# h of the four-block units turned by a DMA transpose on the load queue, in a training step of a gated long convolution

## The chip, the core and the metric

The kernel runs on one core of a Trainium2 chip. The metric is the device time of one execution in microseconds, as the median of the runs. The engines that matter are TensorE (PE: matmuls and transposes, results in PSUM), VectorE (DVE: elementwise work), ScalarE (ACT: activations and most copies out of PSUM), GpSimd (POOL) and SyncE (SP, which here only issues DMAs). SP, ACT and POOL each issue DMAs in the order of their own queue, and a DMA whose condition is not met holds up whatever stands behind it on that queue.

## The reference

The outputs are the forward result and the gradients of all operands of

```
xn  = layernorm(A_q)                                   # 2048 x 1024
kv  = shift_conv(A_k, A_shift_k) * A_v
s   = xn * (long_conv(kv, A_ssm_k) + kv * A_ssm_D)     # FFT convolution over 2048 rows
g   = xn @ w_gate;  u = xn @ w_up;  h = g * u          # 2048 x 3584
bm  = h @ w_down
out = A_q + s * silu(bm)
```

The gradient of w_down needs h with the rows of the sequence on the partitions, and h @ w_down needs h turned, with the features on the partitions. So the kernel writes both forms of h to DRAM: `Hd` as it is computed and `HTd` turned.

## The kernel before, in words

Everything is bf16 with sums in fp32. The 2048 rows are 16 blocks of 128 (`NB`), the 3584 features 14 slabs of 256 (`SLW`, `NSL`).

*The first stage* runs to about 528 us and does two things at once. `gu_unit` computes g and u for one slab and a run of blocks: four blocks in 54 of the units, one or two blocks in six early ones (the first 512 rows of slabs 0 and 1). For each block there are eight matmuls of 128x512 (line 661) that put u and g side by side into one PSUM tile `psg`, and a ScalarE copy to `gut` (line 663). At the end of a unit ScalarE's queue stores `gut` to `GUd` (line 670). Between the blocks the call `tick()` at line 669 emits pieces of `conv_forward`, the long convolution as discrete Fourier transforms: short matmuls into `psF` (line 235) and `psY` (lines 438 and 449), ScalarE copies of `psF` to `SP` (lines 257 and 295), and very much VectorE work (all of it through `tt`, line 213, on tiles W, KX, HX, m, U). How much is emitted at each tick is worked out from estimated VectorE weights, so the order of TensorE's, VectorE's and ScalarE's work is fixed at build time; most of these instructions are pinned to program order. The spectra go to DRAM from GpSimd's queue, `KFd<-KX` among them.

*What happens to h.* In the first block of the next unit `multiply` makes `hN` = u * g on VectorE (line 675; three buffers) and GpSimd's queue stores it to `Hd` (line 676). `multiply` puts `turn` on the list `later`. `flush(5)`, called once per block at line 664, adds one to the age of each entry and runs those that have reached 5. `turn` (lines 685 to 692) turns the eight 128x128 squares of a unit with TensorE against the identity into a PSUM tile (line 690), copies it to `hT` with ScalarE (line 691; two buffers), and `store` writes it to `HTd` on SP's queue (line 682, issued through `ld`, line 61).

*SP's queue* in this stage also carries the slab loads (`wslab`, line 540, two buffers, issued about a slab ahead) and, near the end, the pieces of w_down (`WD[0]` to `WD[6]`, `load_wd`) and the first loads of `HTd`.

*The second stage*, h @ w_down, begins at 519 us with `bm_first` (line 989): TensorE goes over 28 chunks `fc` of 128 features for two row blocks at a time (four matmuls of 128x512 per chunk, line 985); chunk fc reads `WD[fc // 4]`. A flush at line 1002 after its first four chunks runs what is left on `later`. `WD[6]` lies in a buffer of a pool that is allocated only when the pools of the first stage, `hT`'s among them, are released. After each pair of blocks `gate` does the elementwise part (its first VectorE instruction on a result is gg, on bm and sig). Behind this come the two stages of the gate and up gradients, the gradient of w_down and that of the layer norm, up to 1929 us.

Of the kernel before, what the change touches and what calls it, by code (L numbers as in the profile page):

```python
# [19 lines left out]
def build_kernel(  # L20
# [11 lines left out]
    nc = tc.nc  # L32
# [27 lines left out]
    def ld(out, in_):  # L60
        return nc.sync.dma_start(out=out, in_=in_)
# [3 lines left out]
    def st(out, in_):  # L65
        ins = nc.gpsimd.dma_start(out=out, in_=in_)  # L66
        if PINQ[0]:
            tc.keep_in_program_order(ins)
        return ins

    def sta(out, in_):
        return nc.scalar.dma_start(out=out, in_=in_)
# [139 lines left out]
    def tt(o, a, b, op):  # L212
        pinned(V.tensor_tensor(o, a, b, op))  # L213
# [401 lines left out]
    def turn_late():  # L615
        for i, (x, q, qi) in enumerate(turn_rows):
            ps = ps_st.tile([P, DC, P], BF16, name="tr")
            for dc in range(DC):
                tr_ln[0] = nc.tensor.transpose(ps[:, dc, :], x[:, dc * P:(dc + 1) * P], ident[:])
            if i % 2 == 0:  # L620
                act_copy[0] = nc.scalar.copy(out=XNT[q][:, :, qi * P:(qi + 1) * P], in_=ps[:])
            else:
                V.tensor_copy(XNT[q][:, :, qi * P:(qi + 1) * P], ps[:])
        turn_rows.clear()
# [3 lines left out]
    later = []  # L628
    gu_mm = [None]

    def defer(fn):
        later.append([0, fn])

    def flush(age=0):

        for e in later:
            e[0] += 1
        while later and later[0][0] >= age:
            later.pop(0)[1]()
# [5 lines left out]
    def gu_unit(sl, b0, n, w, tick):  # L645

        if n == 4:
            turn_of[0] += 1
            if turn_of[0] % 3 == 0 and sl < NSL - 2:
                gut = U[5][:, 2048:4096].rearrange("p (a i f) -> p a i f", a=2, i=4)  # L650
            else:
                gut = fg.tile([P, 2, 4, SLW], BF16, name="gut")
            hN = fg.tile([P, 2, 4, P], BF16, name="hN", bufs=3)
        else:
            gut = lnp.tile([P, 2, 2, SLW], BF16, name="gut_s", bufs=6)
            hN = lnp.tile([P, 2, 2, P], BF16, name="hN_s", bufs=6)
        for i in range(n):
            q, qi = divmod(b0 + i, 4)
            ps = ps_gu.tile([P, 512], F32, name="psg")
            for dc in range(DC):  # L660
                gu_mm[0] = nc.tensor.matmul(ps[:], XNT[q][:, dc, qi * P:(qi + 1) * P],  # L661
                                            w[:, dc].rearrange("p a f -> p (a f)"), start=(dc == 0), stop=(dc == DC - 1))
            nc.scalar.copy(out=gut[:, :, i], in_=ps[:].rearrange("p (a f) -> p a f", a=2))  # L663
            flush(5)
            if i == 0:
                turn_late()
            hn[0]()
            hn[0] = nop
            tick()
        sta(GUd[sl, b0 // 8][:, :, b0 % 8:b0 % 8 + n], gut[:, :, 0:n])  # L670

        def multiply():
            with tc.issue_after(last.ins) if b0 + n <= 4 and chunk[0] <= 2 else nullcontext():
                by_half = lambda t: t.rearrange("p i (a f) -> p a i f", a=2)
                tt(hN[:, :, 0:n], by_half(gut[:, 0, 0:n]), by_half(gut[:, 1, 0:n]), MUL)
            st(Hd[sl][:, :, b0:b0 + n, :], hN[:, :, 0:n])
            defer(turn)
        hn[0] = multiply

        def store(hT):  # L680
            fr, so = sl % 12 * SLW, b0 % 8 * P
            ld(HTd[b0 // 8][sl // 12][fr:fr + SLW, so:so + n * P].rearrange("(a f) s -> f a s", f=P),
               hT[:, :, 0:n].rearrange("f a i s -> f a (i s)"))

        def turn():
            hT = fg.tile([P, 2, 4, P], BF16, name="hT") if chunk[0] > 5 else lnp.tile([P, 2, 4, P], BF16, name="hT_s", bufs=5)
            ps = ps_tr.tile([P, 2, 4, P], BF16, name="tr")
            for a in range(2):
                for i in range(n):
                    nc.tensor.transpose(ps[:, a, i, :], hN[:, a, i, :], ident[:])  # L690
            nc.scalar.copy(out=hT[:, :, 0:n], in_=ps[:, :, 0:n])
            store(hT)
# [239 lines left out]
    def tick(by=1):  # L932
        cnt[0] += by
        if cnt[0] == -4:
            pump((SHIFT_W + 4.05) / F_TOTAL)
        if cnt[0] >= -2:
            pump((SHIFT_W + (F_TOTAL - SHIFT_W) * (cnt[0] + 6.5) / (NT + 3.5)) / F_TOTAL)
# [265 lines left out]
    def gate(b, ps):  # L1203
# [36 lines left out]
        if b >= 12:  # L1240
            defer(turn)
# [406 lines left out]
```

## Time and profile before

| what | before |
|---|---|
| median of 3 runs | 1930.18 us (1929.89 to 1932.31) |
| the profiled execution, span | 1929.5 us |
| TensorE busy | 1906.4 us, 10843 matmuls and transposes |
| VectorE busy | 1549.6 us |
| ScalarE busy | 638.4 us |
| GpSimd busy | 330.5 us |
| DMA moved | 444 MB, mean 230 GB/s |

The page cuts the span into 40 slices of 48 us. A digit is the busy share of a slice in tenths; the first 11 slices are the first stage.

```profile
PE   8999999999999999999999999999999999999999
DVE  9999999999937556888899999999996404288884
ACT  5764555555422233343222222222212102011113
PEclk9999999999999999999999999999999999999999
DMA  8876866758899997666788788575787999889985
```

The turning itself appears on the page in these DMA issues (out<-in, queue, count, KB each, median us from issue to landing):

```profile
Hd<-hN POOLq DMA_DIRECT2D x54, 256.0 KB, 4.0
ht<-HTd SPq DMA_DIRECT2D x6, 1536.0 KB, 11.4
```

A matmul is counted as busy for its whole length although the next one starts before it ends: the 128x512 matmuls last 379 ns each and start 216 ns apart when nothing holds them up.

### The profile page before, as it was taken

To read this page: it belongs to the slowest core of one execution; us is meant where nothing else is said; L and a number is where in the kernel's file an instruction comes from. 1 tells how busy PE (TensorE), PEld (TensorE's weight loads), DVE (VectorE), ACT (ScalarE), POOL (GpSimd) and SP (SyncE) were. 2 spreads that over 40 slices of the span, in tenths; PEclk is the share of its full clock that TensorE was granted. 3 is DMA by queue.
4 is the path that set the end of the run, shared out by engine and by line. 5 is a ranking of instruction groups with operands and counts; after the bars stand their busy time and mean duration, and the time that the engine had idled before them with its cause. 6 is when DMAs were issued, how large, how long until landed. Compare 5 with 4: busy or idle time off the path is not lost.

```text
span 1929.5 us, 27354 instructions
## 1 busy us (share of the span) xinstructions
PE 1906.4 (99%) x10843; PEld 1031.0 (53%) x10978; DVE 1549.6 (80%) x1730; ACT 638.4 (33%) x942; POOL 330.5 (17%) x461
## 2 busy tenths in 40 slices
PE   8999999999999999999999999999999999999999
PEld 5555555555444456665666666664444444444444
DVE  9999999999937556888899999999996404288884
ACT  5764555555422233343222222222212102011113
POOL 4121212111112210000122131121211101011111
PEclk9999999999999999999999999999999999999999
DMA  8876866758899997666788788575787999889985
GB/s 293 268 259 217 261 209 226 234 196 268 272 270 311 282 313 258 208 202 219 258 246 261 239 248 262 202 272 174 226 253 174 157 205 210 153 170 201 191 177 169
DMA packets 451361, 444.43 MB, mean 230 GB/s; under 512 B 268801, under 2 KB 371613, under 8 KB 436769
## 3 DMA queue, kind: packets, MB, share of 16 engines
q1 hardware_dynamic: 394848, 243.36, 48.0%
q0 software_dynamic: 40064, 169.95, 27.8%
q10 hardware_dynamic: 16320, 29.36, 4.2%
q8 instruction: 86, 1.41, 0.3%
q14 instruction: 43, 0.34, 0.1%
HBM read 194.00 MB, written 185.64 MB: 197 GB/s over the span
## 4 chain that ended last, share of the span: by engine, by line
PE 71%; DVE 18%; DMA 4%; issue 4%; ACT 1%; SPq 1%; POOL 0%; DVEq 0%; ACTq 0%; POOLq 0%
PE psb L1356 20%; PE psb L1339 10%; PE psbm L985 10%; PE psx L1486 10%; PE psb L1434 9%; PE psg L661 6%; DVE W L213 4%; DVE KX L213 2%; DVE HX L213 2%; PE psF L235 2%; DVE dkp L1184 2%; DVE m L213 1%; DVE U L213 1%; DMA dkT<-DKSHd 1%; DVE hN L213 1%
## 5 line engine op out<-in xcount | busy, mean ns | idle before, releaser
L661 PE MATMUL psg<-wslab,U 128*128 128x512 bf16 x1733 | 401.6, 379 | 4.8 <-ACT U L597 1.0
L1356 PE MATMUL psb<-U,U 128*128 128x512 bf16 x1792 | 397.0, 379 | 0.0
L1486 PE MATMUL psx<-U,dgut 128*128 128x512 bf16 x1505 | 331.2, 379 | 2.4 <-DMA dgut<-DGd 0.8
L1486 PEld LDWEIGHTS <-dgut 128*128 128x128 bf16 x1792 | 175.2, 98 | 212.5 <-DMA dgut<-DGd 1.3
L1356 PEld LDWEIGHTS <-U 128*128 128x128 bf16 x1792 | 175.3, 98 | 197.9
L661 PEld LDWEIGHTS <-U 128*128 128x128 bf16 x1792 | 172.5, 98 | 187.3 <-issue 1.8
L1339 PE MATMUL psb<-wdt,U 128*128 128x256 bf16 x1792 | 205.6, 273 | 0.0
L1339 PEld LDWEIGHTS <-U 128*128 128x128 bf16 x1792 | 175.3, 98 | 29.2
L1434 PE MATMUL psb<-U,U 128*128 128x512 bf16 x797 | 175.9, 379 | 0.9
L213 DVE TENSOR_TENSOR W<-W 128x1024 f32<-128x1024 f32 (+1 forms) x174 | 171.6, 1003 | 3.7
L1361 ACT CAST wb<-psb 128x512 bf16<-128x512 f32 x112 | 65.6, 586 | 315.4 <-PE psb L1356 307.3
L985 PE MATMUL psbm<-U,ht 128*128 128x512 bf16 x658 | 144.8, 379 | 0.7
L1434 PEld LDWEIGHTS <-U 128*128 128x128 bf16 x896 | 87.5, 98 | 104.5
L663 ACT CAST gut<-psg 128x512 bf16<-128x512 f32 x156 | 91.6, 588 | 120.8 <-PE psg L661 118.9
L1518 ACT ACTIVATE dx_t<-dxn 128x1024 bf16<-128x1024 f32 x15 | 15.9, 1058 | 325.5 <-DVE dxn L213 325.5
L1184 DVE SCALAR_TENSOR_TENSOR dkp<-dkT,kT 128x1024 bf16<-128x1024 bf16 (+2 forms) x64 | 78.4, 1224 | 39.9 <-DMA dkT<-DKSHd 37.9
L985 PEld LDWEIGHTS <-ht 128*128 128x128 bf16 x672 | 65.7, 98 | 78.6
L213 DVE TENSOR_TENSOR U<-U,dht 128x2048 bf16<-128x2048 bf16 x56 | 68.3, 1221 | 46.4 <-ACT dht L1341 46.4
L1341 ACT CAST dht<-psb 128x512 bf16<-128x512 f32 x112 | 65.7, 587 | 116.3 <-PE psb L1339 116.3
L66 POOL DMA_DIRECT2D Hd<-hN x54 | 37.0, 685 | 292.9 <-DVE hN L213 291.8
L213 DVE TENSOR_TENSOR dxn<-psx,dxna_t 128x1024 f32<-128x1024 f32 x15 | 18.3, 1222 | 79.5 <-PE psx L1486 75.4
L1465 ACT CAST wbs<-psb 128x512 bf16<-128x512 f32 x51 | 29.9, 586 | 145.3 <-PE psb L1434 134.3
(260 smaller groups left out, 2464.6 us busy)
## 6 DMA issues: line engine op xcount, KB each, us to landing
U<-GUd SPq DMA_DIRECT2D x28, 1024.0 KB, 7.7
DGd<-U SPq DMA_DIRECT2D x28, 1024.0 KB, 6.0
GUd<-gut ACTq DMA_DIRECT2D x39, 512.0 KB, 6.0
out_dram<-wb SPq DMA_DIRECT2D x112, 128.0 KB, 3.9
U<-Hd SPq DMA_DIRECT2D x14, 1024.0 KB, 6.0
Hd<-hN POOLq DMA_DIRECT2D x54, 256.0 KB, 4.0
HTd<-hT SPq DMA_DIRECT2D x52, 256.0 KB, 3.9
ht<-HTd SPq DMA_DIRECT2D x6, 1536.0 KB, 11.4
```

The costliest lines, as they stand in the source:

```text
L213: pinned(V.tensor_tensor(o, a, b, op))
L235: mm = nc.tensor.matmul(ps[:, k].rearrange("p (c d) -> p c d", c=2), T[:, r, k, :], xr[:, r], start=(n == 0), stop=(n == len(rs) - 1 and ( ...
L661: gu_mm[0] = nc.tensor.matmul(ps[:], XNT[q][:, dc, qi * P:(qi + 1) * P], w[:, dc].rearrange("p a f -> p (a f)"), start=(dc == 0), stop=(dc ...
L663: nc.scalar.copy(out=gut[:, :, i], in_=ps[:].rearrange("p (a f) -> p a f", a=2))
L985: mm = nc.tensor.matmul(ps[:, dh * 512:(dh + 1) * 512], ht(fc)[:, i * P:(i + 1) * P], WD[fc // 4][:, fc % 4, dh * 512:(dh + 1) * 512], sta ...
L1184: ins = V.scalar_tensor_tensor(prod[:].rearrange("p r d -> p (r d)")[:, lo:H], dkT[:, 0, lo:H], 1.0, kT[:, 0, 13 + m + lo:13 + m + H], op0 ...
L1339: nc.tensor.matmul(ps[:, x * SLW:(x + 1) * SLW], DBMT[2 * hf + g][:, dc, (b % 4) * P:(b % 4 + 1) * P], wdt[:, dc, :], start=(dc == 0), sto ...
L1341: nc.scalar.copy(out=dht[:, 2 * e:2 * e + 2].rearrange("p b f -> p (b f)"), in_=ps[:])
L1356: nc.tensor.matmul(ps[:], XN[b // 4][:, b % 4, dc * P:(dc + 1) * P], dgus[b // 8][:, :, b % 8], start=(b == 0), stop=(b == NB - 1))
L1361: nc.scalar.copy(out=wb[:, dc % 2].rearrange("p a f -> p (a f)"), in_=ps[:])
L1434: nc.tensor.matmul(ps, h[:, f, b, :], DBM[b // 4][:, b % 4, dh * 512:(dh + 1) * 512], start=(b == 0), stop=(b == NB - 1))
L1486: nc.tensor.matmul(ps[:, dh * 512:(dh + 1) * 512], t[n][:, f, i * P:(i + 1) * P], WGU[n][:, f, dh * 512:(dh + 1) * 512], start=(n == 0 and ...
```

## The change

For a unit of four blocks `turn` issues one DMA transpose on SP's queue, from `hN` straight to `hT`, both in SBUF, and puts the store on the list `later` by itself. The eight TensorE transposes and the ScalarE copy of such a unit are gone. `defer` takes a starting age: `turn` of a four-block unit starts at 3 and so runs two blocks after `multiply` instead of five; the store starts at 2 and runs three blocks after that. Units of one and two blocks stay as they were.

```diff
-    def defer(fn):
-        later.append([0, fn])
+    def defer(fn, age=0):
+        later.append([age, fn])
...
             st(Hd[sl][:, :, b0:b0 + n, :], hN[:, :, 0:n])
-            defer(turn)
+            defer(turn, 3 if n == 4 else 0)
...
         def turn():
             hT = fg.tile([P, 2, 4, P], BF16, name="hT") if chunk[0] > 5 else lnp.tile([P, 2, 4, P], BF16, name="hT_s", bufs=5)
+            if n == 4:
+                nc.sync.dma_start_transpose(out=hT[:].rearrange("p a i s -> p (a i) s"),
+                                            in_=hN[:].rearrange("p a i f -> p (a i f)"))
+                defer(lambda: store(hT), 2)
+                return
             ps = ps_tr.tile([P, 2, 4, P], BF16, name="tr")
```

In the built kernel each of the 54 transposes waits for VectorE's hN; the store that follows waits for the transpose to have landed; hN of the unit three later waits for it too. VectorE's instructions stand in the same order as before.

## The prediction

> **What bounds the kernel now.** I read the busy time by stage first, because the share of TensorE over the whole span (99%) hides which engine it waits for. The rows give the stretch, then busy time (and count) of each engine, the clock, the DMA share and GB/s.
>
> ```profile
> core 0: us, PE busy (x) PEld busy (x) DVE busy (x) ACT busy (x) POOL busy (x), PEclk, DMA share, GB/s
> 18.00:60.00 42.00, 39.48 (x265) 20.91 (x268) 41.09 (x99) 31.12 (x46) 19.32 (x27) 1.00 0.90 303
> 60.00:530.00 470.00, 461.12 (x2829) 258.12 (x2883) 465.05 (x424) 264.07 (x371) 78.81 (x111) 1.00 0.72 239
> 530.00:554.00 24.00, 23.84 (x126) 12.44 (x128) 0.42 (x2) 5.63 (x8) 1.15 (x1) 1.00 0.88 230
> 554.00:718.00 164.00, 163.21 (x764) 75.11 (x778) 105.41 (x167) 46.52 (x46) 38.11 (x60) 1.00 1.01 298
> ```
>
> The turning of h happens before 530 us. There VectorE is as full as TensorE: 465 of 470 us, and what is missing is mostly the step from one instruction to the next. From 18 to 530 us I find two real VectorE waits, 0.22 and 0.46 us. From 530 us on VectorE is empty until 554 us and has slack to 718 us; there TensorE alone sets the time. So two engines are full up to 530 us, and work taken from one of them is worth only what the other lets through. The clock is 1.00 throughout.
>
> Next the groups that the change removes, then the timeline at the places that decide. The last number in brackets is the idle time before the instruction and who ended it.
>
> ```profile
> L690 PE MATMUL tr<-ident,hN 128*128 128x128 bf16 x432 | 33.1, 219 | 1.9 <-DVE hN L213 1.7
> L691 ACT COPY hT<-tr 128x1024 bf16<-128x1024 bf16 x52 | 53.0, 1018 | 6.6 <-PE tr L690 6.6
> ```
>
> ```profile
> 113.65 1.23 DVE L213 TENSOR_TENSOR KX<-KX,HX 128x2048 bf16<-128x2048 bf16 x1 [0.22 <-DMA KFd<-KX]
> ...
> 391.28 0.61 PE L690 MATMUL tr<-ident,hN 128*128 128x128 bf16 x8
> 391.73 0.59 PE L661 MATMUL psg<-wslab,U 128*128 128x512 bf16 x2
> ...
> 477.52 1.93 ACT L295 COPY SP<-psF 128x1024 f32<-128x1024 f32 x2 [0.43 <-DVE W L213]
> ...
> 492.17 0.62 PE L690 MATMUL tr<-ident,hN 128*128 128x128 bf16 x8 [1.71 <-DVE hN L213]
> ...
> 522.74 0.68 DVE L213 TENSOR_TENSOR hN<-gut 128x1024 bf16<-128x1024 bf16 x1
> 524.59 0.61 PE L690 MATMUL tr<-ident,hN 128*128 128x128 bf16 x8
> 530.49 0.37 SPq L61 DMA_DIRECT2D U<-in_B_w_down_dram  x1
> ...
> 554.00 0.69 DVE L213 TENSOR_TENSOR gg<-bm,sig 128x1024 bf16<-128x1024 bf16 x1 [23.58 <-ACT sig L1217]
> ```
>
> At 477.52 ScalarE's copy of a transform half waits for VectorE: the last place where TensorE's own order (its psF tiles, line 295) is tied to VectorE. At 492.17 TensorE waits for VectorE's hN itself. At 530.49 the load of the seventh w_down piece (WD[6]) goes out.
>
> **The change, part by part.**
>
> *Removed from TensorE.* A unit's eight transposes hold it from 391.28 to 391.73: 0.45 us. The before program has 432 of them, 54 units: 24.3 us. Nearly all of it lies beside VectorE. To count what reaches the path I start at the last tie, 477 us: whatever TensorE saved before it is spent waiting for VectorE's W there. After it there are seven groups of L690 (482.26, 486.60, 492.17, 508.18, 515.53, 522.88, 524.59): 7 x 0.45 = 3.15 us, and the wait of 1.87 us before 492.17 (490.08 to 492.17 between matmul starts, less the running one) goes too, since TensorE no longer reads the hN of these units. Together 5.0 us. From below 0, if a load is late; from above 24.3 us, if VectorE did not bind.
>
> *Removed from ScalarE.* 54 copies of 1.018 us, 55 us. ScalarE is busy 264 of 470 us, so this costs and gives nothing; its cover is that idle 206 us. If ScalarE were the limit it would be worth up to 55 us.
>
> *Added: 54 DMA transposes of 256 KB on SP.* SBUF to SBUF is not in the trace. The nearest rows are transposes of the same 256 KB out of DRAM, dgut and kT, and the smallest and largest of 168 dgut landings:
>
> ```profile
> dgut<-DGd SPq DMA_TRANSPOSE x168, 4.2
> kT<-in_A_k_dram SPq DMA_TRANSPOSE x16, 3.8
> HTd<-hT SPq DMA_DIRECT2D x52, 256.0 KB, 3.9
> U<-in_B_w_down_dram SPq DMA_DIRECT2D x1, 1024.0 KB, 5.5
> DMA to landing us min/median/max: 2.5/4.2/18.4
> ```
>
> The fourth row is from 523 to 531 us, the last is dgut's. So 2.5 to 18.4 us, and I take 4.0, between the two medians of equal size. The issue itself takes SP 1.2 us (median 1226 ns of line 1429). Engine time: between 1524 and 1660 us queue q1 took 86.8% of 136 us, 118 us, for 46 dgut, 7 transposes of 1 MB and 4 of 256 KB, 78 quarter megabytes, so 1.5 us each. Fifty-two more in 470 us are 78 us, 17%, on a DMA share of 0.72: 0.89, full but not over.
>
> The Trainium skill speaks against the change here: "VectorE: DVE Perf Modes", section "The three transpose paths", lists 390 ns for a 128x128 tile on TensorE and 1309 ns by DMA, and its rules send a 128x128 turn to TensorE wherever PSUM will do. The trace has TensorE at 56 ns a tile when eight follow each other (0.45 us / 8), and DMA at 4.2 us for 256 KB, eight such tiles. By the page a unit taken as eight DMA tiles in a row would need, as an estimate, 10.5 us; SP would then miss the pace of a unit (worked out below) by 2.1 us, 51 times, less 16.5 us of slack, and the sum would be some 2020 us. By the row it is the forecast.
>
> *The new wait on SP.* The store HTd<-hT stood behind ScalarE's copy; now it stands behind the landing of its transpose on the same queue, and behind it wait the next transpose, the slab loads, WD[3] to WD[6] and the loads of HTd. Per unit SP is held 4.0 + 0.36 (store) + 0.26 (a quarter of a slab's two issues, 0.37 and 0.65 us) = 4.6 us, against 9.06 us per unit ((522.74 - 60.47) / 51). The slab loads are issued about a slab (36 us) ahead and land in 8.6 us: no cost, and up to 4.6 us each if that lead were gone. hN has three buffers, so VectorE's next-but-two hN waits for a landing, 27 us later. In the built program GUd stores on ScalarE's queue wait for DMAs about three units older, some 25 us: no cost while SP keeps pace.
>
> *The end of the stage.* Here it does cost. WD[6] waits for the last store of hT to land, since its buffer lies over hT's. Before: hN done 523.4, transposes, copy, store at 526.3, landed about 530.4, load at 530.49, landed 530.49 + 5.5 = 536.0. After: 523.4 + 4.0 (transpose) + 3.9 (store) + 0.2 (two issues) = 531.5, and + 5.5 = 537.0. TensorE reaches fc 24, which reads WD[6], at 519.43 + 96 x 0.2155 + 2 x 0.45 = 541.0 before, and 5.0 us earlier, at 536.0, after. It waits 1.0 us: the gain is 541.0 - 537.0 = 4.0 us. By the ends: 5.0 us with 3.0 us or less for the transpose, 0 with 8.0 us, a loss of 10.4 us with 18.4.
>
> *DMA contention on VectorE.* The KX store, issued at 107.44, lands just too late already (the 0.22 us at 113.65). One transpose ahead of it costs between 0 and 1.5 us of engine time; as VectorE is full, that goes to the end. I take 0.7. No other VectorE instruction of the stage waits for a DMA.
>
> **Sum.** -4.0 + 0.7 = -3.3 us, against the profiled 1929.5: 1926.2. The median of the runs is 0.7 us above the profile, so 1926.9.
>
> **Rivals.**
>
> *TensorE is the real limit* and the full 24.3 us come back: 1930.2 - 24.3 = 1905.9. For it: TensorE busy 461 of 470 us. Against: VectorE's 465 and its two waits in 512 us.
>
> *The SP queue becomes the limit* (slower). From a landing of 8.4 us on, 8.4 + 0.62 = 9.06, the queue no longer keeps a unit's pace; the backlog goes into hN's 27 us, then into VectorE. At 9.0 us: 0.56 x 51 = 28.6 us, less the 18 us of slack left, 10.6 us: 1940.8. For it: landings of up to 18.4 us, 8.0 for the 512 KB wdt transposes, a stage that already has a DMA share of 0.72 to 0.90, and SBUF as source unseen. Against: the medians of 3.8 and 4.2 us were taken at shares of 0.86 to 1.06.
>
> *The head start is given back*: 1930.2. From 554 to 718 us the DMA share is 1.01; if loads, not TensorE, paced that stage, 4 us at its start vanish. Against: TensorE is busy 163.2 of 164 us there, and ht is loaded a pair (24 us) ahead.
>
> *The change does not take effect*: excluded by the order of the built kernel, which has 864 TensorE instructions fewer and VectorE's in the same order.
>
> **How the numbers follow.** Forecast (0 to 5 us gained) 0.54, TensorE the limit 0.08, SP the limit 0.23, given back 0.15. The forecast's own range is 1925.2 to 1930.2, plus a little either way. A measurement of this kernel tells 0.2%, 3.9 us, from no change: below 1926.3 or above 1934.0. The forecast's value lies near that edge: I put 0.29 of its 0.54 below, 0.23 within, 0.02 above. With the first rival, faster is 0.37; with 0.13 of the fourth case, same is 0.36; slower is 0.23 + 0.02 + 0.02 = 0.27. Below 1923.5 lies mostly the first rival (0.08), above 1938 about half of the SP rival (0.12): the range is 1923.5 to 1938.
>
> **What would show it.** Right: VectorE still without a wait up to about 530 us, TensorE with new waits behind psF copies between 60 and 480 us that eat some 20 us, transposes landing in about 4 us, WD[6] landing near 537, gg near 550. Wrong: VectorE waiting for a transpose (hN in its idle time), SP held by landings of 8 us or more, TensorE waiting for wslab, or a stage that ends 15 us earlier or more.

## The result, and the profile after

The changed kernel took 1962.72 us in the median of four runs (1954.22 to 1975.46), the kernel before 1930.25 beside it: ratio 1.0168, 95% interval 1.0139 to 1.0198. It is slower by 32 us, above the range of the prediction (1923.5 to 1938). The profiled execution has a span of 1967.9 us. The 40 slices of its page, now of 49 us each, show first where to look: VectorE's second slice and TensorE's clock in it.

```profile
DVE  9699999999937554888799989999998212378884
...
PEclk9799999999999989999999999999999999999999
DMA  9989999998999999565877888765787999889985
```

The table by stage of the changed kernel (stretch, then busy time and count of each engine, granted clock, DMA share, GB/s) says how much.

```profile
core 0: us, PE busy (x) PEld busy (x) DVE busy (x) ACT busy (x) POOL busy (x), PEclk, DMA share, GB/s
18.00:60.00 42.00, 40.01 (x271) 21.11 (x270) 34.79 (x96) 31.35 (x46) 18.37 (x25) 1.00 0.92 253
60.00:100.00 40.00, 23.21 (x107) 12.07 (x106) 27.00 (x18) 16.18 (x20) 5.02 (x7) 0.66 0.91 213
100.00:560.00 460.00, 438.88 (x2394) 231.54 (x2393) 445.06 (x410) 199.25 (x298) 75.11 (x106) 0.99 0.97 260
560.00:600.00 40.00, 33.97 (x167) 16.45 (x166) 13.70 (x22) 12.80 (x14) 6.21 (x9) 0.91 0.96 278
600.00:757.00 157.00, 147.31 (x691) 67.08 (x690) 91.70 (x145) 39.33 (x39) 33.02 (x52) 0.97 1.06 276
```

VectorE, which was full, has lost some 19 us before 100 us: 34.8 of 42 and 27.0 of 40. From 18 to 60 us the DMA engines moved 253 GB/s instead of 303, at a share that hardly differs (0.92 and 0.90). TensorE, idle in pieces, was granted 0.66 of its clock from 60 to 100 us. VectorE's timeline shows the two waits (start, length, instruction, idle time before it and who ended it):

```profile
53.00 0.68 DVE L174 TENSOR_SCALAR mm<-mm 128x1024 int32<-128x1024 int32 x1
63.23 2.29 DVE L213 TENSOR_TENSOR U<-k,Wbc 128x4096 bf16<-128x4096 bf16 x1 [9.54 <-DMA U<-in_A_v_dram]
...
82.08 0.69 DVE L213 TENSOR_TENSOR hN<-gut 128x1024 bf16<-128x1024 bf16 x1
91.77 2.36 DVE L213 TENSOR_TENSOR W<-SP 128x1024 f32<-128x1024 f32 x2 [9.01 <-ACT SP L295]
```

The first wait is for the loads of k and v, which the short convolution needs: one of the k loads took 21.3 us to land, where those of before took 9.6 to 11.1. The second is for a ScalarE copy. SP's timeline and then ScalarE's and TensorE's show what stood before that copy:

```profile
40.43 3.00 SPq L688 DMA_TRANSPOSE hT_s<-hN  x1
44.16 18.56 SPq L61 DMA_DIRECT2D HTd<-hT_s  x2
62.81 5.24 SPq L688 DMA_TRANSPOSE hT_s<-hN  x1
77.27 0.36 SPq L61 DMA_DIRECT2D HTd<-hT_s  x1
77.73 1.29 SPq L688 DMA_TRANSPOSE hT_s<-hN  x1
83.19 0.36 SPq L61 DMA_DIRECT2D HTd<-hT_s  x1
83.64 0.61 SPq L540 DMA_DIRECT2D wslab<-in_B_w_up_dram  x1
```

```profile
89.81 1.93 ACT L295 COPY SP<-psF 128x1024 f32<-128x1024 f32 x2 [12.66 <-DMA wslab<-in_B_w_up_dram]
```

```profile
90.88 1.01 PE L235 MATMUL psF<-hx,TF 128*128 128x256 bf16 x4 [10.96 <-ACT SP L295]
```

The first transpose goes out at 40.43 us; the store of its hT, the second of the two in the next row, leaves only at the row's end, 62.7, when the transpose has landed. SP reaches the third slab's load at 83.64 us instead of 64.34. ScalarE copies nothing for 12.66 us until that load lands, TensorE waits 10.96 us for ScalarE, VectorE 9.01 us. A chain through four engines starts at a queue that the prediction had put at no cost.

Line 688 of the changed kernel, which issues the transposes (count, then shortest, median and longest time of the issue in ns, and below it from issue to landing):

```profile
L688 SPq DMA_TRANSPOSE hT<-hN x51: 1232/1554/11610, 86.6 to 555.0; - x51
...
DMA to landing us min/median/max: 3.1/6.0/21.9
```

At the end of the stage SP's queue holds up WD[6] as well, in SP's timeline and TensorE's:

```profile
545.33 4.15 SPq L688 DMA_TRANSPOSE hT<-hN  x1
...
554.58 0.36 SPq L61 DMA_DIRECT2D HTd<-hT  x1
555.04 1.25 SPq L688 DMA_TRANSPOSE hT<-hN  x1
558.76 0.36 SPq L61 DMA_DIRECT2D HTd<-hT  x1
561.41 0.37 SPq L61 DMA_DIRECT2D U<-in_B_w_down_dram  x1
```

```profile
566.98 3.52 PE L990 MATMUL psbm<-U,U 128*128 128x512 bf16 x8 [6.04 <-DMA U<-in_B_w_down_dram]
```

The last hN is done at 545.9 us, but the last transpose only leaves at 555.04, since the one before it took 9.25 us to land (545.33 to the store at 554.58). From the last hN to the use of WD[6] it is 21.1 us, where the prediction had 13.6 (523.4 to 537.0).

### The profile page after: what moved, and what is told of

Same layout as the page of the kernel before. It is cut to its first block, busy times and chain, and to the rows that moved or that the text cites. A ratio compares the mean times of both kernels' runs of the same rounds, so it can differ in the third digit from the quotient of the medians.

```text
span 1967.9 us, 26629 instructions
## 1 busy us (share of the span) xinstructions
PE 1905.5 (97%) x10546; PEld 1012.9 (51%) x10546; DVE 1550.1 (79%) x1730; ACT 589.9 (30%) x888; POOL 329.9 (17%) x461
## 2 busy tenths in 40 slices
DMA packets 508380, 458.52 MB, mean 233 GB/s; under 512 B 325824, under 2 KB 428636, under 8 KB 493792
## 4 chain that ended last, share of the span: by engine, by line
PE 65%; issue 12%; DVE 5%; DMA 4%; SPq 2%; POOL 1%; ACT 0%; POOLq 0%; ACTq 0%; DVEq 0%
PE psb L1361 20%; PE psx L1491 20%; PE psb L1344 10%; PE psb L1439 9%; DMA yf_t<-YFd 2%; PE psg L661 2%; PE psbm L990 2%; DVE W L213 1%; SPq L1250 1%; PE psF L235 1%; DVE HX L213 1%; PE psY L438 1%; POOL Hd L66 1%; DMA hT<-hN 1%; PE psY L1137 1%
## 5 line engine op out<-in xcount | busy, mean ns | idle before, releaser
L661 PE MATMUL psg<-wslab,U 128*128 128x512 bf16 x1792 | 407.6, 383 | 7.2 <-ACT gut L663 4.3
L213 DVE TENSOR_TENSOR W<-SP 128x1024 f32<-128x1024 f32 x64 | 74.4, 1220 | 10.5 <-ACT SP L295 9.6
```

## The experiments

"Units" are the 54 units of four row blocks, in their order of time. All times are medians; the ratio is to the kernel before, run beside it.

| run | turned by DMA | us | ratio, 95% interval |
|---|---|---|---|
| changed kernel | all 54 | 1962.72 | 1.0168 (1.0139 to 1.0198) |
| g0_after_again | all 54 | 1964.59 | 1.0163 (1.0121 to 1.0205) |
| h2_first_two_only | first 2 | 1942.18 | 1.0058 (1.0043 to 1.0073) |
| e2_start_only | first 10 | 1950.88 | 1.0109 (1.0094 to 1.0124) |
| e3_end_pe | first 46 | 1956.68 | 1.0137 (1.0122 to 1.0152) |
| e1_start_pe | last 44 | 1939.77 | 1.0044 (1.0027 to 1.0060) |
| g2_middle_only | 36 in the middle | 1930.34 | 1.0007 (0.9992 to 1.0021) |
| g3_every_other | 18 of these 36 | 1930.39 | 0.9997 (0.9989 to 1.0006) |
| g1_five_late | 6 of the last 8 | 1932.30 | 1.0011 (1.0003 to 1.0020) |
| h3_end_but_two | all but first 10, last 2 | 1941.0 | 1.0070 (1.0044 to 1.0097) |
| h1_all_but_two_and_end | all but first 2, last 8 | 1946.45 | 1.0082 (1.0060 to 1.0105) |
| i1_gu_by_pool | as h1, GUd from GpSimd | 1932.23 | 1.0026 (1.0004 to 1.0048) |
| i2_before_gu_by_pool | none, GUd from GpSimd | 1934.65 | 1.0021 (1.0012 to 1.0030) |
| e4_no_turn | none, no turning | 1925.35 | 0.9969 (0.9953 to 0.9985) |
| f1_plain_copy | none, 54 plain copies | 1930.63 | 0.9993 (0.9981 to 1.0004) |
| f2_store_later | all 54, store later | 1968.17 | 1.0188 (1.0163 to 1.0213) |
| f3_extra_transposes | 52 beside TensorE's | 1954.09 | 1.0119 (1.0071 to 1.0168) |

### Where the loss is made

Most of the runs choose the units by a condition in `gu_unit`, the others go through TensorE as before:

```diff
     def gu_unit(sl, b0, n, w, tick):
+        by_dma = n == 4 and sl > 2
...
-            defer(turn, 3 if n == 4 else 0)
+            defer(turn, 3 if by_dma else 0)
...
-            if n == 4:
+            if by_dma:
                 nc.sync.dma_start_transpose(...)
```

That is e1_start_pe.

> Slabs 0 to 2 (the first 10 units of four row blocks, up to about 100 us) are turned by TensorE again, the other 44 by DMA. Theory 1 (the loss is made at the start, where SP's transposes hold up SP's other work, ScalarE waits behind a store, and VectorE gets 9.5 + 9.0 us late): VectorE loses less than 4 us before 100 us, and the time is 1936 to 1945 instead of about 1962. Theory 2 (every transpose costs, evenly over the stage): 32 x 44/54 = 26 us stay, about 1956. Theory 3 (TensorE, with less to do, loses its clock over the whole stage): about 1956 too, with the granted clock below 1.00 through the stage.

e2_start_only: `by_dma = n == 4 and sl <= 2`.

> The counterpart: only the first 10 units (slabs 0 to 2) by DMA, the other 44 by TensorE. Theory 1: the 18.5 us of VectorE waits before 100 us are there again, 1945 to 1955. Theory 2 and theory 3: 32 x 10/54 = 6 us, about 1936. In both the stage from 100 us on is as before, without a VectorE wait.

e3_end_pe: `by_dma = n == 4 and sl < NSL - 2`.

> The last 8 units (slabs 12 and 13) by TensorE, so that the buffer under WD[6] comes free as early as before; the other 46 by DMA. Theory 4 (the end of the stage and the stage behind it make the loss: WD[6] late, TensorE idle 6.2 us, its clock at 0.91 after it): the 6.2 us at fc 24 and the low clock go, 8 to 15 us less than the changed kernel, 1948 to 1955. Theories 1 and 2: within 5 us of the changed kernel, 1957 to 1965.

e1 gave 1939.77, without a VectorE wait over 0.3 us before 100 us; e2 gave 1950.88, with waits of 10.86 and 6.77 us there. Both fall where theory 1 had them; ten units cost 20 us, and theory 2 had 6 for them. e3 lies just outside both of its ranges (1956.68), 6 us below the changed kernel. The two intervals overlap, so e3 alone doesn't show a price of the end; the end is taken up again below.

e1 also shows what the prediction had listed as a sign of being wrong: VectorE waiting for a transpose. SP's timeline and then VectorE's:

```profile
502.94 9.72 SPq L689 DMA_TRANSPOSE hT<-hN  x1
```

```profile
519.91 0.69 DVE L213 TENSOR_TENSOR hN<-gut 128x1024 bf16<-128x1024 bf16 x1 [5.08 <-DMA hT<-hN]
```

The issue alone of that transpose held SP for 9.72 us, and hN's three buffers were used up. TensorE waited another 3.3 us for WD[6] in this run.

g2_middle_only (`2 < sl < NSL - 2`) and g3_every_other (`... and b0 % 8 == 0`) ask whether the middle costs anything, and g1_five_late (`sl >= NSL - 2 and (b0, sl) < (12, NSL - 2)`) whether the predicted gain can be had alone. g0 repeats the changed kernel.

> Slabs 3 to 11 by DMA (36 units, about 100 to 470 us), the start and the end by TensorE. If the loss is made of places (start 20 us, end some 7 us, middle 0 to 5 us): last hN within 5 us of before (522.7), gg within 6 of 554, 1929 to 1936. If every transpose costs alike: 32 x 36/54 = 21 us, about 1951.

> Every other unit of the same slabs 3 to 11 (18 units) by DMA. DMA share of 100 to 500 us about 0.82 instead of 0.72 (none) and 0.93 (all). If what decides is how full the 16 DMA engines are: no VectorE wait over 1 us and 1927 to 1931. If each transpose costs alike: half of what the 36 of the middle cost.

> Only six units are turned by DMA, those of slabs 12 and 13 but for the last two, hN between about 475 and 515 us, where the DMA share of before is lowest; the last two by TensorE, so that WD[6] is not late. The step of the prediction that TensorE's saving pays only after its last tie to VectorE at 477 us, as a term by itself: six groups of 0.45 us and part of the 1.87 us wait, 2 to 4 us less than before, 1926 to 1928.5. If six transposes cost more than they save: 1931 or more.

> The changed kernel once more, unaltered, because its times lie far apart (1954 to 1975) and its profile has a wait of 9.8 us at 717 us, behind the last turning, that no other profile here has. If that wait is chance: from the first gg to the end of w_down 164.5 us as in all other runs (176.5 in the first profile), the last hN at 540 to 552 us, gg 575 to 586, 1950 to 1975. If it belongs to the change: 176 us again.

The 36 transposes of the middle cost nothing: 1930.34. Its table by stage, in its profiled execution (which was 14 us longer than the median for a wait behind this stage; see the last section):

```profile
100.00:500.00 400.00, 379.43 (x2130) 206.49 (x2169) 395.75 (x355) 190.73 (x281) 69.20 (x98) 0.99 0.92 261
```

VectorE is as full as ever (395.75 of 400) at a DMA share of 0.92, so a share near 0.9 by itself is no loss. They also gain nothing, although TensorE lost its turning of 36 units: VectorE still sets the pace. g1, against its expectation, was 1.9 us slower instead of 2 to 4 faster. TensorE did end its part of the stage 3.0 us earlier there (its first matmul of the second stage, into psbm, at 516.4 instead of 519.4), but then waited 3.50 us for the hN of the last two units, which VectorE made no sooner. g0 came back at 1964.59 with 164.5 us from the first gg to the end of w_down, so the wait at 717 us is not in every execution; the last section comes back to it. Two other points of its expectation were missed: the last hN came at 560.4 us and the first gg at 592.4, later than the ranges (540 to 552, 575 to 586). Against before, 37 us were lost by the last hN here and 22.5 in the first profile of the same kernel, so where the loss falls differs from execution to execution.

### What a transpose does to the others

> The turning of the 54 units is left out: hN itself is stored where hT was, so TensorE and ScalarE lose the same work as in the changed kernel, and no DMA transpose is there. Theory 3 (what hurts is TensorE's missing work, by its clock): 1940 or more. Theories 1, 2, 4 (what hurts is the transposes): not slower than before, 1922 to 1930; VectorE still full to 530 us, so not the 24.3 us of TensorE's work.

```diff
-                nc.sync.dma_start_transpose(out=hT[:]..., in_=hN[:]...)
-                defer(lambda: store(hT), 2)
+                defer(lambda: store(hN), 2)
```

Without the turning of the 54 units the time is 1925.35, 5.2 us less than before. TensorE's missing work is therefore not the harm, and theory 3 falls. VectorE in its profile, from the table by stage:

```profile
60.00:530.00 470.00, 446.98 (x2417) 238.30 (x2463) 465.46 (x424) 215.19 (x317) 78.54 (x111) 0.98 0.73 239
```

465.46 of 470 us, as before (465.05): of the 24.3 us taken off TensorE only about 5 came back, as much as the prediction counts behind the last tie. That they come from there is not shown: the profiled execution is one of the slower ones of e4 (span 1927.4), and its first gg comes 2.5 us earlier than before (551.48 instead of 554.00).

> Each of the 54 DMA transposes becomes a plain DMA copy of the same 256 KB from hN to hT, on the same queue in the same place, waited for in the same way: the turning is left out. Theory 5 (the price is what a transpose takes of the 16 DMA engines and takes from the other transfers): the copies land in 2 to 4 us, no VectorE wait over 1 us, 1925 to 1933. Theory 6 (the price is SP held by the store that waits for a landing, whatever lands): 1940 to 1955, with SP held some 150 us in all.

```diff
-                nc.sync.dma_start_transpose(out=hT[:]..., in_=hN[:]...)
+                ld(hT[:].rearrange("p a i s -> p (a i s)"), hN[:].rearrange("p a i f -> p (a i f)"))
```

> All 54 DMA transposes stay. Only the store of each hT is put behind the next unit's transpose on SP, one unit (9 us) later, so that SP rarely stands at a landing. Theory 6: SP's waits for hT<-hN fall from 227 us to below 60, the third slab's load goes out before 75 us instead of 83.6, and the time falls by 10 us or more, to 1932 to 1950. Theory 5: the v load still lands late, VectorE's waits before 100 us stay above 10 us, and the time is 1952 to 1968.

```diff
-                nc.sync.dma_start_transpose(out=hT[:]..., in_=hN[:]...)
-                defer(lambda: store(hT), 2)
+                ins = nc.sync.dma_start_transpose(out=hT[:]..., in_=hN[:]...)
+                if late:
+                    with tc.issue_after(ins.ins):
+                        late.pop()()
+                late.append(lambda: store(hT))
```

> The kernel before, with TensorE turning as it did, and 52 DMA transposes of hN besides, into the hT of the unit before, which has been stored by then. No store waits for them; only ScalarE's copy into that buffer does, a unit later. Theory 5: the transposes slow the loads beside them whoever waits for them, VectorE loses 5 us or more before 100 us, 1940 to 1960. Theory 6: 1930 to 1936.

```diff
             store(hT)
+            if n == 4:
+                if spare[0] is not None and spare[0][0] == (chunk[0] > 5):
+                    nc.sync.dma_start_transpose(out=spare[0][1][:]..., in_=hN[:]...)
+                spare[0] = (chunk[0] > 5, hT)
```

f1 is the sharpest. The same bytes on the same queue, with SP held for 210 us in all by stores that wait for a landing (186.7 + 23.3; 227 + 30 with transposes), and the time is 1930.63. Three VectorE waits are left in the start, 1.09, 1.87 and 0.54 us, a little more than expected, and the copies land in 4.2 us (the transposes in 6.0). Theory 6 falls as far as the sum goes: SP can be held that long in all without harm. In the start f1 also held it for less (the first copies landed in 11.5 and 12.8 us, the third slab's load went out at 71.0 us instead of 83.6), so f1 does not test what a lateness of 19 us there costs. f2 says less than it was meant to. SP's waits for a transpose fell to 3.2 us and the third slab's load went out at 75.0, but the transposes now waited 183 us for stores out of hT's two buffers. What it does show is that VectorE's first wait stayed (9.34 us) whatever SP did behind the first transpose. Its second one grew to 13.56 us although the slab load was earlier: ScalarE now stood 11.62 us until a store of hT_s on SP's queue had landed. The time was 1968.17. f3 costs 23 us though nothing but a later copy waits for its transposes; but its first one went out at 63.4 us, behind the k and v loads, and VectorE lost just 0.6 us before 100 us. Its time fits theory 5, the place that theory 5 had named does not. The trace shows a direct wait in its place: from 100 to 560 us ScalarE's copies into hT stood 26.7 us in all, nine times, until a transpose had landed, and VectorE's longest waits (4.55 and 3.88 us before the hN at 493.80 and 512.80) are for ScalarE right behind two of these. So f3 does not show transfers slowed by transposes.

What a transpose does that a copy doesn't is read from the DMA queues between 52 and 62 us, while the first transpose is in flight (in f1 it is the second copy): packets and MB, then the load queue q0, which carries k and v (packets, MB, share of the 16 engines). First before, then the changed kernel, then f1:

```profile
DMA packets 1551, 3.86 MB, mean 386 GB/s; under 512 B 195, under 2 KB 607, under 8 KB 1421
...
q0 software_dynamic: 667, 2.61, 67.9%
```

```profile
DMA packets 1211, 2.32 MB, mean 232 GB/s; under 512 B 553, under 2 KB 631, under 8 KB 1174
...
q0 software_dynamic: 480, 1.81, 75.4%
```

```profile
q0 software_dynamic: 673, 2.70, 73.1%
```

One packet of q0, of 3.8 to 4.0 KB in all three, takes 0.163 us of an engine before (0.679 x 160 us / 667), 0.174 beside a plain copy, and 0.251 beside a transpose, 1.5 times as long. That is an average: the harm lies at its start. The same rows from 50 to 54 us, with SP's queue q1, in the same order:

```profile
q0 software_dynamic: 318, 1.09, 85.7%
q1 hardware_dynamic: 261, 0.13, 14.0%
```

```profile
q0 software_dynamic: 94, 0.36, 92.3%
q1 hardware_dynamic: 249, 0.06, 33.8%
```

```profile
q0 software_dynamic: 259, 0.87, 82.6%
q1 hardware_dynamic: 164, 0.16, 20.2%
```

There a packet of q0 takes 0.63 us (0.923 x 64 us / 94) instead of 0.17, and 0.20 beside the copy; from 58 to 62 us it is back at 0.19 (0.18 before). The transpose's own time adds to it (q1 took 46.1% from 46 to 50 us, 1.8% before). What inside the DMA engines makes the other packets slower no run here tells. A transpose is cut small: the whole program has 57,023 more packets under 512 B (325,824 against 268,801), 1056 for each. The Trainium skill says in "DMA: Bandwidth & Descriptors", section "Rules for kernel authors", that DMAs of different issuing engines share the same 16 DMA engines and interleave; the trace agrees, since the queue that suffers is GpSimd's and the transpose is SP's.

### Which of the first ten, and how it spreads

h2_first_two_only: `by_dma = n == 4 and b0 == 4 and sl < 2`. h1_all_but_two_and_end: `n == 4 and (b0 != 4 or sl > 1) and sl < NSL - 2`. h3_end_but_two: `n == 4 and sl > 2 and (b0, sl) < (12, NSL - 2)`.

> Two of the 54 units only are turned by DMA, the first two (row blocks 4 to 7 of slabs 0 and 1), whose transposes go out at 40 and 63 us; 52 by TensorE. Theory 7 (the place decides: a transpose beside the k and v loads, at a DMA share over 1): VectorE waits some 9 us at 54 us for k and v, 1938 to 1950. Theory 8 (what decides is SP held by one transpose after the other ahead of the third slab's load): the wait at 54 us is below 4 us, 1930 to 1935.

> The reverse: the first two by TensorE, and the last eight (slabs 12 and 13), the other 44 by DMA. Theory 7: no VectorE wait over 2 us before 100 us, 1929 to 1936. Theory 8: half or more of the 20 us of the start remain, 1940 to 1950.

> The first ten and the last two units by TensorE, the 42 between by DMA. If the price of the end (1939.8 with the last eight by DMA, 1930.3 with none of them) is that of the last two, whose store WD[6] waits for: 1929 to 1933. If it is the eight's load on the DMA engines beside the loads of w_down: 1935 to 1940.

h2 costs 11.9 us. VectorE's timeline has it in one line:

```profile
65.48 2.29 DVE L213 TENSOR_TENSOR U<-k,Wbc 128x4096 bf16<-128x4096 bf16 x1 [11.02 <-DMA U<-in_A_v_dram]
```

The second transpose goes out at 64.96 us, when most of this wait is over, so the 11 us belong to the first. Two units of 54 make a third of the loss. h1, all the others without the end, still costs 16 us, though VectorE waits nowhere for 2 us before 100 us: one half of theory 7 and one of theory 8. Its waits (who waits, for what; total, times, longest) are later, from 100 to 560 us:

```profile
ACT SP L257 <- DMA wslab<-in_B_w_up_dram: 12.1, 1, 12.1
...
ACT yf L771 <- DMA wslab<-in_B_w_up_dram: 6.9, 1, 6.9
```

Again ScalarE stands still until a slab load has landed, which it does not read. The two waits end at 147 and 382 us, in the stretch where the same transposes cost nothing in g2; why eight more of them (the third to the tenth unit) bring the waits there is not shown. In the built program the DMAs of SP's and of ScalarE's queue count on the same eight semaphores in turn, so a GUd store on ScalarE's queue waits for DMAs that SP issued before, and ScalarE's copies stand behind the store. The last two runs take this store out of ScalarE's queue.

> As h1 (44 units by DMA, the first two and the last eight by TensorE), and the GUd stores of the four-block units are issued by GpSimd instead of ScalarE. Theory 9 (ScalarE's queue, held by a GUd store until a slab load has landed, passes SP's lateness on to TensorE and VectorE): ScalarE's waits of 12.1 and 6.9 us for wslab are gone, 1930 to 1937 instead of 1946.5. Theory 10 (the DMA engines are simply too full for 44 transposes): 1941 to 1952 as before.

> The kernel before with the same move of the GUd stores to GpSimd's queue and no transposes: what the move costs by itself. Both theories: 1928 to 1934.

```diff
-        sta(GUd[sl, b0 // 8][:, :, b0 % 8:b0 % 8 + n], gut[:, :, 0:n])
+        (st if n == 4 else sta)(GUd[sl, b0 // 8][:, :, b0 % 8:b0 % 8 + n], gut[:, :, 0:n])
```

i1 came to 1932.23, from 1946.45, with the same transposes, though four of its ten runs still took 1937.5 to 1947.8. The tables by stage of h1 and then i1:

```profile
100.00:530.00 430.00, 396.20 (x2193) 211.57 (x2191) 408.69 (x371) 190.64 (x283) 72.17 (x102) 0.97 0.96 252
```

```profile
100.00:530.00 430.00, 410.73 (x2290) 219.72 (x2289) 423.85 (x383) 197.72 (x291) 105.65 (x151) 0.98 0.95 264
```

At the same DMA share (0.96 and 0.95) VectorE is full again, 423.85 instead of 408.69 us, and no ScalarE wait for wslab is left. Theory 9 holds for the most part, theory 10 falls. The move by itself costs 4.3 us (i2, a little above its range), so it is no gain for the kernel before.

h3 did not settle the end. Its four runs lie at 1929.0, 1940.1, 1941.9 and 1950.6, its profiled execution at a span of 1927.2 without a VectorE wait over 0.5 us. Whether the price of the end is that of the last two units is left open. No kernel that turns all of h was faster than the kernel before by more than its interval.

## Why the prediction was wrong, point by point

Adding units in their order gives the bill: the first 2 cost 11.9 us, the first 10 20.3, the first 46 26.1, all 54 32. These prices don't add up one by one (h1 without the first two and the last eight still costs 16 us), and the four runs of all 54 lie 21 us apart.

**TensorE's saving: right in size.** The prediction had 5.0 us of 24.3, counted from the last tie at 477 us; with the turning left out (e4) it was 5.2. The size agrees; the place is not traced, and the units of slabs 12 and 13 but for the last two, by themselves (g1), gained nothing. **ScalarE's 55 us:** nothing came back, as it said.

**"The DMA share 0.89, full but not over": wrong, in two ways.** The engine time of one transpose was mis-sized: from 100 to 500 us queue q1 took 45.2% after and 23.3% before, 87.6 us for 43 transposes, 2.0 us each instead of 1.5 (a plain copy: 0.7), and the share became 0.97. That did little (g2). The larger fault is that the share was an average over 470 us, while the first transpose goes out before the range it was taken over, into a stretch where the DMA engines were already full (1.03 from 50 to 60 us before). There it landed after 22 us and not 4, and the transfers beside it ran slower. Over the whole stage the median landing was 6.0 us instead of 4.0.

**"No other VectorE instruction of the stage waits for a DMA": true of the trace of before, and the wrong question.** The instruction on k at 53.74 us did not wait, but the last of the four k loads went out at 41.8 us and took 11.1 us to land, so by this estimate k was there at 52.9, with 0.8 us of slack. This step priced contention at 0.7 us; with the first two units alone (h2) VectorE waited 11.02 us there and the time rose by 11.9. A transfer that nobody waits for has to be given its slack, not a zero.

**"No cost" for SP and "no cost while SP keeps pace" for ScalarE's stores: wrong.** The steady sum (4.6 of 9.06 us per unit) did no harm in the middle by itself (g2); in the start SP reached the third slab's load 19.3 us late, more than half the slab's lead. The condition on ScalarE's stores was seen and named, and then taken as met; with the stores off ScalarE's queue (i1) 14 of h1's 16 us are gone.

**The end:** a gain of 4.0 us was predicted, and WD[6] came 21.1 us after the last hN instead of 13.6. Of the 7.5 us too many, the wait for the transpose before the last, still not landed, explains 9.1, and the shorter store takes some back (2.7 instead of 3.9). The last transpose itself took 3.7, near the 4.0. With the last eight by DMA (e1) the loss is 9.2 us; with these on TensorE (g2) it is none. How much of it is the last two units' is open (h3).

**The rival "the SP queue becomes the limit"** had the sign, with a chance of 0.23. But its mechanism, a landing above 8.4 us at the steady pace of 9.06, was not what happened: the median landing was 6.0, and f1, where SP waits nearly as long, loses nothing. The rival "head start given back" wasn't reached, as there was no head start.

The page of the Trainium skill that spoke against the change, "VectorE: DVE Perf Modes", was right here in its advice (section "Rules for kernel authors": TensorE for a 128x128 transpose where PSUM will do as its destination). The estimate of 10.5 us per unit from the figure in its section "The three transpose paths" is above the median landing of 6.0 us here, and the runs put much of the harm in the transfers beside a transpose.

## What to carry to other kernels

Before adding a DMA, look at the fullest ten microseconds in which it will run, not at the stage's mean share, and list every load in flight there with the time between its landing and its first use. A DMA transpose is not a copy: here one of 256 KB cost 11 us in a full stretch, and 36 cost nothing in a stretch where loads had slack (g2), but gained nothing either. An in-order queue passes lateness to whatever shares its semaphores: in h1 a store in ScalarE's queue stopped ScalarE's copies for up to 12.1 us while a DMA of SP's queue was late.

## What was not expected of the hardware

The time that SP needs to issue one DMA transpose ranged from 1.2 to 20 us in these runs. The kernel before already has such transposes in the stage behind (U<-DBMd). SP's timeline of before, then of the profiled execution of g2 (span 1942.7 us, median of its runs 1930.3):

```profile
683.62 7.02 SPq L1288 DMA_TRANSPOSE U<-DBMd  x1
```

```profile
688.91 19.97 SPq L1294 DMA_TRANSPOSE U<-DBMd  x1
```

Behind the second one the loads for the next row block wait, VectorE stands 16.1 us for yf, and TensorE 9.2 us for dbm: the stretch from the first gg to the end of w_down took 176.6 us instead of 164.5. In the first profile of the changed kernel it is a transpose of w_down that took 15.0 us to issue, with the same wait at 717 us; g0 had neither.

Where TensorE stood idle, its clock was lower as well: in the changed kernel 60 to 100 us was granted 0.66. Its 128x512 matmuls start 0.43 us apart instead of 0.216 at 78 us already, before the wait of 10.96 us, and again behind it, and are back at 0.216 from 96 us on. What this costs beside the wait itself was not tried.
